# Where the low part of a weight lies in its slot: 2048 instead of 4096 bytes behind the high part, in a float32 attention and feed-forward kernel

## The chip, the cores and the metric

The kernel runs on one core of one Trainium2 chip. The metric is the device time of one execution in microseconds (us); the median of several executions counts, and less is better.

## The reference

`q`, `k`, `v` are float32 of shape (8, 8, 576, 64): batch, heads, sequence, head size. Attention is done in chunks of 64 rows with nothing between chunks. Its result, put together over heads, is the input of a two-layer feed-forward net whose weights are float64.

```python
scores = (1 / sqrt(64)) * q_c @ k_c.T          # per batch, head and chunk: 64 x 64
attn = exp(scores - scores.max(-1)); attn /= attn.sum(-1) + 1e-9
x = (attn @ v_c)  -> (4608, 512)               # tokens x (heads * head size)
h = x @ w_in                                   # w_in (512, 2048)
g = h / (1 + exp(-1.702 * h))
out = (g @ w_out).astype(float32)              # w_out (2048, 512)
```

## The kernel before

**Tiles.** The 4608 tokens are 36 tiles of 128, taken in 9 blocks (`NB`) of 4 tiles (`BT` = 512 tokens). The 2048 inner columns are 16 slices (`NF`) of 128. So the feed-forward net has 144 steps g = (block n, slice j).

**High and low parts.** Every matrix that goes into a feed-forward matmul is split into a high part (the value in the short float form `float32r`) and a low part (what the high part leaves over). A product is then three matmuls: high times low, high times high, low times high. In a step g there are 12 matmuls for `hp` (four chunks `cc` of the 512 input features, three each, lines 606 to 608; the slice of `w_in` is the stationary operand, `x_l` or `x_h` the moving one, 128x512) and 12 for `po` (four token tiles t, three each, lines 641 to 643; `g_l` or `g_h` is stationary, the slice of `w_out` moves, 128x512). For the very first step `h_half` (lines 619 to 621) does the `hp` part in two halves of 256 tokens.

**Which line reads which part.** Line 606 has the high part of `w_in` as stationary operand (moving `x_l`), 607 the same high part (moving `x_h`), 608 the low part (moving `x_h`). Lines 641 and 642 move the high part of `w_out` (stationary `g_l`, `g_h`), 643 moves the low part (stationary `g_h`).

**Weight slots.** There are 16 slots of 8192 bytes per partition, one for each slice j, and they hold the weights for the whole run. The slices j of `w_in` and `w_out` arrive as raw float64 words in the slot (`load`), are turned into float32 in a scratch tile `wtmp` (ScalarE at lines 172 and 176, VectorE at 181, 182 and 188), and then ScalarE writes the high parts into the slot (`part_h`, line 193) and VectorE the low parts (`part_l`, line 196). This is done 16 times, between 28.8 and 119 us of the profile.

**Order.** A planner (`Plan`) sets the order of all instructions from costs, ranks and needs that stand in `plan.add` calls; the order is fixed when the program is built. Within an engine instructions run in that order. The attention of later tiles is slipped in between feed-forward steps. While PE (TensorE's matmuls) runs one matmul, PEld (its weight load) loads the stationary operand of the next.

**After the matmuls.** ScalarE computes g in place in PSUM (line 627) and its high part (628), VectorE the low part (632); at the end of a block the four `po` tiles go to SBUF (lines 650 and 652) and out.

Of the kernel before, what the change touches and what calls it, by code (L numbers as in the profile page):

```python
# [9 lines left out]
F32 = mybir.dt.float32  # L10
F32R = mybir.dt.float32r
# [3 lines left out]
AF = mybir.ActivationFunctionType  # L15
# [83 lines left out]
def tile_chunk_attention_ffn(  # L99
# [9 lines left out]
    nc = tc.nc  # L109
# [4 lines left out]
    P = 128  # L114
    CH = 64
    NP = H // 2
    NCC = DM // P
# [11 lines left out]
    const = ctx.enter_context(tc.tile_pool(name="const", bufs=1))  # L129
# [14 lines left out]

    wt, w_raw, w_tmp = {}, {}, {}

    def slot_user(j):

        return divmod(NF - 1 - j, 2)

    def plan_w(j):
        rank = 0.986 * j - 3.0

        def words():
            word = lambda t, i: w_raw[j].bitcast(t).rearrange("p (n w) -> p n w", w=2)[:, :, i]
            return word(F32, 1), word(I32, 1), word(I32, 0), word(U32, 0)

        def load(part):  # L160
            if part == 0:
                w_raw[j] = const.tile([P, 1024], I64, tag=f"w{j}", name=f"raw_{j}")
                nc.sync.dma_start(  # L163
                    w_raw[j][:, :512].rearrange("p (cc f) -> p cc f", cc=NCC),
                    w_in[:, j * P : (j + 1) * P].rearrange("(cc p) f -> p cc f", p=P),
                )
            else:
                nc.sync.dma_start(w_raw[j][:, 512:], w_out[j * P : (j + 1) * P, :])  # L168

        def scale():  # L170
            hf, hi, li, lu = words()
            nc.scalar.activation(hf, hf, AF.Copy, scale=2.0**-112)  # L172

        def low():
            hf, hi, li, lu = words()
            nc.scalar.activation(li, lu, AF.Copy, scale=2.0**-29)

        def high():
            hf, hi, li, lu = words()
            w_tmp[j] = tmp = more.tile([P, 1024], I32, tag="wtmp", name=f"wtmp_{j}")  # L180
            nc.vector.tensor_scalar(tmp, hi, 3, None, op0=ALU.logical_shift_left)
            nc.vector.scalar_tensor_tensor(
                tmp, hi, -(2**31), tmp, op0=ALU.bitwise_and, op1=ALU.bitwise_or
            )

        def join():
            hf, hi, li, lu = words()
            nc.vector.tensor_tensor(w_tmp[j], w_tmp[j], li, op=ALU.add)
            w_raw.pop(j)

        def part_h():
            wt[j] = const.tile([P, 2, 1024], F32R, tag=f"w{j}", name=f"w_{j}")
            nc.scalar.activation(wt[j][:, 0, :], w_tmp[j].bitcast(F32), AF.Copy)

        def part_l():
            nc.vector.tensor_tensor(  # L196
                wt[j][:, 1, :],
                w_tmp.pop(j).bitcast(F32),
                wt[j][:, 0, :].bitcast(F32),
                op=ALU.subtract,  # L200
            )

        u, kind = slot_user(j)
        need = [f"{('s', 'xp')[kind]}_{u}"] if u < TB else []
        e = lambda n: f"{n}_{j}"
        plan.add(DMA, 1.6, rank - 5.5, lambda: load(0), need=need, make=e("rawi"), take=[f"w{j}"])
        plan.add(DMA, 1.6, rank - 5.5, lambda: load(1), need=[e("rawi")], make=e("raw"))
        plan.add(ACT, 1.1, rank, scale, need=[e("raw")], make=e("wsc"))
        plan.add(ACT, 1.1, rank, low, need=[e("wsc")], make=e("wlow"))
        plan.add(DVE, 1.95, rank, high, need=[e("wsc")], make=e("whigh"), take=["tmp"])  # L210
        plan.add(DVE, 1.25, rank, join, need=[e("whigh"), e("wlow")], make=e("wj"))
        plan.add(ACT, 1.05, rank - 3.5, part_h, need=[e("wj")], make=e("wh"))
        plan.add(DVE, 1.25, rank - 2, part_l, need=[e("wh")], make=e("w"), give=["tmp"])


# [372 lines left out]
    def plan_ffn(g):  # L588
        n, j = divmod(g, NF)
# [8 lines left out]
        def h_pe(half):  # L598
            if half == 0:
                h_t[g] = ps_h.tile([P, BT], F32, tag="hp", name=f"hp_{g}")  # L600
            hp = h_t[g]
            w = wt[j][:, :, :512].rearrange("p w (cc f) -> p w cc f", cc=NCC)
            for cc in range(2 * half, 2 * half + 2):
                wh, wl = w[:, 0, cc, :], w[:, 1, cc, :]
                xh, xl = x_h[n][:, cc, :], x_l[n][:, cc, :]
                nc.tensor.matmul(hp, wh, xl, start=cc == 0, stop=False)  # L606
                nc.tensor.matmul(hp, wh, xh, start=False, stop=False)  # L607
                nc.tensor.matmul(hp, wl, xh, start=False, stop=cc == NCC - 1)  # L608

        def h_half(half):  # L610
            if half == 0:
                h_t[g] = ps_h.tile([P, BT], F32, tag="hp", name=f"hp_{g}")
            c = slice(half * BT // 2, (half + 1) * BT // 2)
            hp = h_t[g][:, c]
            w = wt[j][:, :, :512].rearrange("p w (cc f) -> p w cc f", cc=NCC)
            for cc in range(NCC):
                wh, wl = w[:, 0, cc, :], w[:, 1, cc, :]
                xh, xl = x_h[n][:, cc, c], x_l[n][:, cc, c]
                nc.tensor.matmul(hp, wh, xl, start=cc == 0, stop=False)
                nc.tensor.matmul(hp, wh, xh, start=False, stop=False)  # L620
                nc.tensor.matmul(hp, wl, xh, start=False, stop=cc == NCC - 1)
# [11 lines left out]

        def o_pe(t):
            gh, gl = g_t[g]
            w = wt[j][:, :, 512:]
            if j == 0:
                po_t[(n, t)] = ps_o.tile([P, DM], F32, tag=f"po{t}", name=f"po_{n}_{t}")
            po = po_t[(n, t)]
            c = slice(t * P, t * P + P)  # L640
            nc.tensor.matmul(po, gl[:, c], w[:, 0, :], start=j == 0, stop=False)  # L641
            nc.tensor.matmul(po, gh[:, c], w[:, 0, :], start=False, stop=False)  # L642
            nc.tensor.matmul(po, gh[:, c], w[:, 1, :], start=False, stop=j == NF - 1)  # L643
# [19 lines left out]
        if g == 0:  # L663
            plan.add(
                PE, 1.37, g - 0.2, lambda: h_half(0), need=[need[0], "xl_0", "xl_1"], make=ev("h0"), take=["hp"]
            )
            plan.add(PE, 1.37, g - 0.2, lambda: h_half(1), need=[ev("h0"), "xl_2", "xl_3"], make=ev("h"))
        else:
            plan.add(PE, 1.37, g - 0.2, lambda: h_pe(0), need=need, make=ev("h0"), take=["hp"])
            plan.add(PE, 1.37, g - 0.2, lambda: h_pe(1), need=[ev("h0")], make=ev("h"), give=last)  # L670
        plan.add(ACT, 1.18, g - 5, g_hi, need=[ev("h")], make=ev("gh"), take=["g"], table="gelu")
        plan.add(DVE, 0.69, g - 5, g_lo, need=[ev("gh")], make=ev("gl"), give=["hp"])
        for t in range(TB):
            po = [f"po{t}"] if j == 0 else []
            plan.add(
                PE, 0.69, g + 2.5, lambda t=t: o_pe(t), need=[ev("gl"), f"w_{j}"]
                + ([f"o_{g - 1}_{t}"] if j else [])
                + ([f"o_{g}_{i}" for i in range(t)] if t == TB - 1 else []),
                make=f"o_{g}_{t}", take=po, give=["g"] if t == TB - 1 else [],
            )  # L680
            if j == NF - 1:
                eng = ACT if t % 2 == 0 else DVE
                tag = ob_tag(t)
                plan.add(
                    eng, 0.6, g - 1, lambda t=t: o_out(t), need=[f"o_{g}_{t}"],
                    make=f"ob_{n}_{t}", take=[tag], give=[f"po{t}"],
                )
                plan.add(
                    DMA, 0.8, g - 20, lambda t=t: o_store(t), need=[f"ob_{n}_{t}"],
                    make=f"st_{n}_{t}", give=[tag],  # L690
                )
# [52 lines left out]
```

## Time and profile before

| | |
|---|---|
| time, median of 3 runs | 889.74 us (889.12 to 889.91) |
| the profiled execution's own time | 889.83 us |
| its span | 888.1 us, 14202 instructions |
| PE busy | 870.6 us (98%), 5882 matmuls |
| VectorE (DVE) busy | 389.8 us (44%) |
| ScalarE (ACT) busy | 317.6 us (36%) |
| GpSimd (POOL) busy | 32.4 us (4%) |
| granted TensorE clock | 0.992 over the span |

A row of the groups reads: line, engine, operation, what it writes <- what it reads, shapes, count | busy us, mean ns of one | idle time of the engine before it and what ended it. A row of the timeline reads: start us, length us, engine, line, operation. The length of a matmul runs from its start to a modelled end, and matmuls overlap: the distance from one start to the next is the pace of the engine.

### The profile page before, as it was taken

How to read it: one execution, taken by the hardware profiler on the slowest of the kernel's cores; microseconds unless marked ns; L12 is line 12 of the kernel's file. 1: busy time of each engine (PE TensorE's matmuls, PEld its weight loads, DVE VectorE, ACT ScalarE, POOL GpSimd, SP SyncE). 2: the span in 40 equal slices, each digit the busy share in tenths (PEclk: the TensorE clock that was granted, in tenths of full speed). 3: DMA queues.
4: the chain of work that ended last, by engine and by line, in shares of the span. 5: the costliest groups of instructions: out<-in, count | busy, mean ns of one | idle time of the engine just before them, and what ended most of it. 6: DMA issues, size and time to landing. Idle time of an engine off the chain costs nothing.

```text
span 888.1 us, 14202 instructions
## 1 busy us (share of the span) xinstructions
PE 870.6 (98%) x5882; PEld 705.6 (79%) x5882; DVE 389.8 (44%) x511; ACT 317.6 (36%) x459; POOL 32.4 (4%) x24
## 2 busy tenths in 40 slices
PE   6799999999999999999999999999999999999998
PEld 5587888888888888888888888888888888888886
DVE  5899975277716153433535171617151411111111
ACT  3999653253423223232423241324232322222221
POOL 1000000011000000000000000000000000000000
PEclk9699999999999999999999999999999999999999
DMA  9995244233442313221222031102010110001001
GB/s 238 311 323 169 47 73 98 38 54 67 82 86 54 54 25 76 45 48 25 69 39 49 16 92 25 25 1 71 2 25 1 32 40 1 0 1 48 1 0 48
DMA packets 194592, 55.47 MB, mean 62 GB/s; under 512 B 179680, under 2 KB 187872, under 8 KB 194528
## 3 DMA queue, kind: packets, MB, share of 16 engines
q1 hardware_dynamic: 194528, 54.57, 26.3%
q8 instruction: 46, 0.75, 0.4%
q14 instruction: 18, 0.15, 0.1%
HBM read 45.09 MB, written 9.44 MB: 61 GB/s over the span
## 4 chain that ended last, share of the span: by engine, by line
PE 94%; SPq 2%; DMA 2%; ACT 1%; issue 0%; DVE 0%; ACTq 0%
PE po L641 16%; PE po L642 15%; PE po L643 15%; PE hp L608 15%; PE hp L607 15%; PE hp L606 15%; PE s L443 2%; PE x L503 2%; SPq L231 1%; DMA raw<-in_moe_w_in_dram 1%; DMA rows<-in_k_dram 1%; ACT raw L172 0%; PE qkTp L410 0%; SPq L168 0%; SPq L163 0%
## 5 line engine op out<-in xcount | busy, mean ns | idle before, releaser
L632 DVE TENSOR_TENSOR g_l<-hp,g_h 128x512 fp32r<-128x512 f32 x144 | 99.3, 690 | 413.3 <-ACT g_h L628 412.7
L641 PE MATMUL po<-w,g_l 128*128 128x512 f32 x576 | 232.1, 403 | 0.1
L628 ACT ACTIVATE g_h<-hp 128x512 fp32r<-128x512 f32 x144 | 86.3, 599 | 404.3 <-PE po L643 403.6
L642 PE MATMUL po<-w,g_h 128*128 128x512 f32 x576 | 227.7, 395 | 0.0
L643 PE MATMUL po<-w,g_h 128*128 128x512 f32 x576 | 227.7, 395 | 0.0
L608 PE MATMUL hp<-x_h,w 128*128 128x512 f32 x572 | 225.2, 394 | 0.0
L607 PE MATMUL hp<-x_h,w 128*128 128x512 f32 x572 | 223.9, 391 | 0.0
L606 PE MATMUL hp<-x_l,w 128*128 128x512 f32 x572 | 223.9, 391 | 0.0
L643 PEld LDWEIGHTS po<-w,g_h 128*128 128x128 f32 x576 | 108.6, 189 | 26.3
L641 PEld LDWEIGHTS po<-w,g_l 128*128 128x128 f32 x576 | 108.2, 188 | 25.4 <-DVE g_l L632 0.9
L606 PEld LDWEIGHTS hp<-x_l,w 128*128 128x128 f32 x572 | 107.8, 189 | 25.0
L642 PEld LDWEIGHTS po<-w,g_h 128*128 128x128 f32 x576 | 109.0, 189 | 23.5
L607 PEld LDWEIGHTS hp<-x_h,w 128*128 128x128 f32 x572 | 107.4, 188 | 25.1
L608 PEld LDWEIGHTS hp<-x_h,w 128*128 128x128 f32 x572 | 107.3, 188 | 23.6 <-DVE w L196 0.2
L627 ACT ACTIVATE hp<-hp 128x512 f32<-128x512 f32 x144 | 84.3, 585 | 72.6 <-PE hp L608 67.6
L490 DVE STREAM_TRANSPOSE eT<-e 32x512 f32<-32x512 f32 x112 | 78.7, 702 | 21.0 <-PE x L503 17.2
L470 POOL TENSOR_TENSOR e<-e,r 128x1024 f32<-128x1024 f32 x14 | 26.7, 1906 | 611.4 <-DVE r L466 325.5
L425 DVE STREAM_TRANSPOSE qkT<-raw 128x1024 f32<-128x1024 f32 x28 | 34.7, 1241 | 13.8 <-PE s L443 11.3
L515 ACT ACTIVATE x_h<-x 128x512 fp32r<-128x512 f32 x32 | 17.5, 595 | 33.2 <-PE x L503 33.1
L459 ACT ACT_TABLE_LOAD x16 | 20.5, 1283 | 19.0 <-DVE e L456 18.3
L463 DVE TENSOR_REDUCE z<-e 128x16 f32<-128x1024 f32 x16 | 19.5, 1218 | 9.5 <-ACT e L459 8.8
L443 PEld LDWEIGHTS s<-qkT 64*64 64x64 f32 x1024 | 18.2, 135 | 5.8 <-issue 5.8
(64 smaller groups left out, 412.2 us busy)
## 6 DMA issues: line engine op xcount, KB each, us to landing
out_dram<-ob SPq DMA_DIRECT2D x36, 256.0 KB, 2.1
raw<-in_moe_w_in_dram SPq DMA_DIRECT2D x16, 512.0 KB, 7.3
raw<-in_moe_w_out_dram SPq DMA_DIRECT2D x16, 512.0 KB, 8.0
v<-in_v_dram SPq DMA_DIRECT2D x28, 256.0 KB, 3.3
raw<-in_q_dram SPq DMA_DIRECT2D x144, 32.0 KB, 2.1
raw<-in_k_dram SPq DMA_DIRECT2D x144, 32.0 KB, 2.1
raw<-in_q_dram SPq DMA_DIRECT2D x48, 24.0 KB, 1.9
raw<-in_k_dram SPq DMA_DIRECT2D x48, 24.0 KB, 1.9
```

Source lines behind the costliest of these rows:

```text
L425: nc.vector.transpose(st["tr"][:, i].rearrange("p n (t j) -> p (n t) j", j=32), st["raw"][:, i].rearrange("p n t j -> p (n t) j"),)
L443: nc.tensor.matmul(o, tr[r, 0, n, cols], tr[r, 1, n, cols], start=True, stop=True)
L490: nc.vector.transpose(st["et"][po : po + 32, :, 32 * a : 32 * a + 32], st["e"][pi : pi + 32, :, 32 * b : 32 * b + 32],)
L606: nc.tensor.matmul(hp, wh, xl, start=cc == 0, stop=False)
L607: nc.tensor.matmul(hp, wh, xh, start=False, stop=False)
L608: nc.tensor.matmul(hp, wl, xh, start=False, stop=cc == NCC - 1)
L627: nc.scalar.activation(h_t[g], h_t[g], AF.Gelu_apprx_sigmoid)
L628: nc.scalar.activation(gh, h_t[g], AF.Copy)
L632: nc.vector.tensor_tensor(gl, h_t.pop(g), gh.bitcast(F32), op=ALU.subtract)
L641: nc.tensor.matmul(po, gl[:, c], w[:, 0, :], start=j == 0, stop=False)
L642: nc.tensor.matmul(po, gh[:, c], w[:, 0, :], start=False, stop=False)
L643: nc.tensor.matmul(po, gh[:, c], w[:, 1, :], start=False, stop=j == NF - 1)
```

## The change

A slot held, in this order, the high part of the `w_in` slice, the high part of the `w_out` slice, the low part of the `w_in` slice, the low part of the `w_out` slice, 2048 bytes each. Now it holds high `w_in`, low `w_in`, high `w_out`, low `w_out`. So the low part of `w_in` moves from byte 4096 to 2048 of the slot, the high part of `w_out` from 2048 to 4096; the other two stay.

```diff
         def part_h():
-            wt[j] = const.tile([P, 2, 1024], F32R, tag=f"w{j}", name=f"w_{j}")
-            nc.scalar.activation(wt[j][:, 0, :], w_tmp[j].bitcast(F32), AF.Copy)
+            wt[j] = const.tile([P, 2, 2, 512], F32R, tag=f"w{j}", name=f"w_{j}")
+            nc.scalar.activation(wt[j][:, :, 0], w_tmp[j].bitcast(F32).rearrange("p (m n) -> p m n", m=2), AF.Copy)
 
         def part_l():
             nc.vector.tensor_tensor(
-                wt[j][:, 1, :],
-                w_tmp.pop(j).bitcast(F32),
-                wt[j][:, 0, :].bitcast(F32),
+                wt[j][:, :, 1],
+                w_tmp.pop(j).bitcast(F32).rearrange("p (m n) -> p m n", m=2),
+                wt[j][:, :, 0].bitcast(F32),
                 op=ALU.subtract,
             )
...
         def h_pe(half):          # and the same edit in h_half
-            w = wt[j][:, :, :512].rearrange("p w (cc f) -> p w cc f", cc=NCC)
+            w = wt[j][:, 0].rearrange("p w (cc f) -> p w cc f", cc=NCC)
...
         def o_pe(t):
-            w = wt[j][:, :, 512:]
+            w = wt[j][:, 1]
```

In the built program every engine has the same instructions in the same order with the same waits, and all tiles start at the same addresses as before. What differs: the 16 instructions of `part_h` and the 16 of `part_l` write (and `part_l` reads) two pieces of 512 elements, 4096 bytes apart, where they wrote 1024 in one run; and 1732 matmuls have another operand address: 1152 (lines 641 and 642) of the moving operand, 580 (lines 608 and 621) of the stationary one. A blank line in the new file moves its later lines by one.

More of the change, by code (lines that the diff above doesn't have):

```diff
@@ L614, in h_half @@
             hp = h_t[g][:, c]
-            w = wt[j][:, :, :512].rearrange("p w (cc f) -> p w cc f", cc=NCC)
+            w = wt[j][:, 0].rearrange("p w (cc f) -> p w cc f", cc=NCC)
             for cc in range(NCC):
```

## The prediction

> **What bounds the kernel now.** I read the page first, for the span and the chain that ended last, and its groups.
>
> ```profile
> span 888.1 us, 14202 instructions
> ...
> PE 94%; SPq 2%; DMA 2%; ACT 1%; issue 0%; DVE 0%; ACTq 0%
> ...
> L632 DVE TENSOR_TENSOR g_l<-hp,g_h 128x512 fp32r<-128x512 f32 x144 | 99.3, 690 | 413.3 <-ACT g_h L628 412.7
> L641 PE MATMUL po<-w,g_l 128*128 128x512 f32 x576 | 232.1, 403 | 0.1
> L628 ACT ACTIVATE g_h<-hp 128x512 fp32r<-128x512 f32 x144 | 86.3, 599 | 404.3 <-PE po L643 403.6
> L642 PE MATMUL po<-w,g_h 128*128 128x512 f32 x576 | 227.7, 395 | 0.0
> L643 PE MATMUL po<-w,g_h 128*128 128x512 f32 x576 | 227.7, 395 | 0.0
> L608 PE MATMUL hp<-x_h,w 128*128 128x512 f32 x572 | 225.2, 394 | 0.0
> L607 PE MATMUL hp<-x_h,w 128*128 128x512 f32 x572 | 223.9, 391 | 0.0
> L606 PE MATMUL hp<-x_l,w 128*128 128x512 f32 x572 | 223.9, 391 | 0.0
> ```
>
> PE carries 94% of the chain, and its six feed-forward lines have no idle time ahead of them (the last column is 0.0 or 0.1 us over hundreds of matmuls). Next came the windows, to see whether that holds in the stretch where weights are still being prepared.
>
> ```profile
> 60.00:80.00 20.00, 20.00 (x92) 16.41 (x91) 18.88 (x23) 18.84 (x22) 0.00 (x0) 1.00 0.88 269
> 80.00:100.00 20.00, 19.69 (x207) 15.48 (x205) 18.36 (x21) 15.44 (x20) 0.00 (x0) 1.00 0.21 37
> ...
> 700.00:800.00 100.00, 100.00 (x491) 81.19 (x490) 19.70 (x30) 23.86 (x41) 0.00 (x0) 1.00 0.04 13
> ```
>
> The columns after the length are the busy time of PE, PEld, DVE, ACT and POOL, then the clock. PE is busy for all of 60 to 80 us and for 19.69 of the next 20, while DVE and ACT are nearly full (18.88 and 18.84 of 20): preparing the weights is hidden, but with little to spare. Late in the run (700 to 800) DVE and ACT are a fifth busy and PE sets the pace alone. The waits of the weight load from 36 us to the end show how little the other engines hold it up (the three rows with another engine in them):
>
> ```profile
> PEld po L641 <- DVE g_l L632: 0.9, 2, 0.6
> PEld qkTp L410 <- ACT eT L481: 0.7, 1, 0.7
> ...
> PEld hp L608 <- DVE w L196: 0.2, 1, 0.2
> ```
>
> That is 1.8 us in all, four waits. So the time is the pace of the matmuls, and the question is whether an operand's address has a say in it. For this the timeline of PE near the end, where one step g follows the other without attention between:
>
> ```profile
> 863.33 0.39 PE L606 MATMUL hp<-x_l,w 128*128 128x512 f32 x1
> 863.55 0.39 PE L607 MATMUL hp<-x_h,w 128*128 128x512 f32 x1
> 863.78 0.39 PE L608 MATMUL hp<-x_h,w 128*128 128x512 f32 x1
> 864.01 0.39 PE L606 MATMUL hp<-x_l,w 128*128 128x512 f32 x1
> 864.24 0.39 PE L607 MATMUL hp<-x_h,w 128*128 128x512 f32 x1
> 864.46 0.40 PE L608 MATMUL hp<-x_h,w 128*128 128x512 f32 x1
> 864.69 0.40 PE L641 MATMUL po<-w,g_l 128*128 128x512 f32 x1
> ...
> 870.25 0.40 PE L641 MATMUL po<-w,g_l 128*128 128x512 f32 x1
> ```
>
> One step of 24 matmuls takes 870.25 - 864.69 = 5.56 us, 231.7 ns each. The `hp` lines run at (864.46 - 863.33)/5 = 226 ns from start to start. The `po` lines run slower; the last stretch of the run, with `po` matmuls alone, shows how:
>
> ```profile
> 875.81 0.40 PE L641 MATMUL po<-w,g_l 128*128 128x512 f32 x1
> 876.05 0.40 PE L642 MATMUL po<-w,g_h 128*128 128x512 f32 x1
> ...
> 877.44 0.40 PE L642 MATMUL po<-w,g_h 128*128 128x512 f32 x1
> 877.68 0.40 PE L643 MATMUL po<-w,g_h 128*128 128x512 f32 x1
> ...
> 879.07 0.40 PE L643 MATMUL po<-w,g_h 128*128 128x512 f32 x1
> 879.31 0.40 PE L641 MATMUL po<-w,g_l 128*128 128x512 f32 x1
> ...
> 880.69 0.40 PE L641 MATMUL po<-w,g_l 128*128 128x512 f32 x1
> 880.93 0.40 PE L642 MATMUL po<-w,g_h 128*128 128x512 f32 x1
> ```
>
> From 875.81 to 880.69 stand 21 steps in 4.88 us: 232.4 ns each, 6.4 more than the `hp` pace. Each pair above is a long one of 0.24 us (0.23 in the unquoted rows between). A long one comes every seventh matmul (1.63, 1.63 and 1.62 us apart), and it falls on line 641, then 642, then 643, then 641 again. So whatever lengthens `po` matmuls goes by a rhythm of its own; it does not stick to the line, though line 643 reads its moving weights 4096 bytes further on in the slot than 641 and 642, and 642's stationary operand lies in another tile than 641's.
>
> **The change part by part.** The order, the waits and the counts stay, so there are two things to price.
>
> First, the 1732 matmuls with another operand address. For the 1152 of lines 641 and 642, the moving weights go from byte 2048 of the slot to 4096. The nearest comparison in this trace is line 642 against line 643: the same stationary `g_h`, the same output, moving weights from byte 2048 against byte 6144. Their means are 395 and 395 ns over 576 each. The rounding leaves half a nanosecond either way: 1152 x 0.5 ns = 0.6 us, gain or loss. For the 580 of lines 608 and 621, the stationary low part goes from byte 4096 to 2048. The nearest comparison is line 607 against 608: the same moving `x_h`, stationary weights from byte 0 against byte 4096: 391 and 394 ns. If the 3 ns were the address, a place nearer to the high part might win or lose up to as much: 580 x 3 ns = 1.7 us either way. The timeline speaks against it: the 608 at 863.78, which another `hp` matmul follows, is 0.39 us long like its neighbours, and the 0.40 us stand at 864.46, where a `po` matmul follows. I take 0 for both, since in the rows nearest to the change an offset of 4096 bytes in the same slot shows nothing.
>
> The Trainium skill has a rule here: SBUF — State Buffer, section "Who interferes with whom", gives PE two independent read ports (moving operand, weight load) and says that PE never waits on anyone; TensorE: Matmul & The Clock Gate, section "Back-to-back issue gap", gives N/2.4 + 2.5 ns from start to start, about 216 ns for 512 columns. By these pages no address could matter and the rivals A and B below would have no chance. The trace does not quite agree with them: 226 and 232.4 ns are 10 and 16 ns above that figure with PE never idle, so something does hold the stream up, and the rivals keep a chance.
>
> Second, the 16 instructions of `part_h` (ACT) and the 16 of `part_l` (DVE) handle two pieces of 512 where they had one run of 1024. The rows for what they cost now, and for a tile written in pieces:
>
> ```profile
> L518 DVE TENSOR_TENSOR x_l<-x,x_h 128x512 fp32r<-128x512 f32 x32 | 20.6, 684 | 2.9 <-ACT x_h L515 2.8
> ...
> L196 DVE TENSOR_TENSOR w<-wtmp,w 128x1024 fp32r<-128x1024 f32 x16 | 19.4, 1215 | 0.4 <-ACT w L193 0.4
> ...
> L515 ACT ACTIVATE x_h<-x 128x512 fp32r<-128x512 f32 x32 | 17.5, 595 | 33.2 <-PE x L503 33.1
> ...
> L193 ACT ACTIVATE w<-wtmp 128x1024 fp32r<-128x1024 f32 x16 | 16.8, 1057 | 0.7 <-DVE wtmp L188 0.7
> ```
>
> Line 518 writes `x_l` in four pieces of 128 with a stride, line 632 writes `g_l` in one run of 512: 684 against 690 ns. On ACT line 515 against line 628: 595 against 599 ns. Pieces cost nothing there, so I take 0 (at best 16 x 6 ns = 0.1 us less). The upper end: if each piece cost as much as an instruction of its own, DVE would pay 2 x 690 - 1215 = 165 ns, 2.6 us in 16, and ACT 2 x 599 - 1057 = 141 ns, 2.3 us in 16. What hides them is PE's own work; only the four waits above (1.8 us) could grow, and from DVE and ACT nearly full at 60 to 80 us I let at most DVE's whole 2.6 us come through.
>
> The sum: 889.83 us (the profiled execution's own time, its span of 888.1 and 1.7 around it) + 0 + 0. This execution lies 0.09 above the median of the runs, 889.74, so I forecast 889.7 us. With the bounds of the matmuls (0.6 and 1.7 us, either way) the likeliest case runs from 887.4 to 892.0, but both ends at once need every bound at its worst; I count within 0.2% (888.0 to 891.5) as this case. About 0.2% is also what a measurement of this kernel can tell from no change, as the three runs already lie 0.8 us apart.
>
> **The rivals.**
>
> A, faster: the `po` matmuls lose their rhythm. They run 6.4 ns above the `hp` pace, and 1152 of the 1728 get another moving address. If these fell to 226 ns, 1152 x 6.4 ns = 7.4 us would go: 882.3 us. For it: the two kinds differ in nothing but operands and addresses, with PE never idle. Against it: the long matmul wanders over all three lines, so the slot offset is not what makes it. Chance 0.09.
>
> B, slower: the reverse, on the `hp` side. While PE streams `x_h`, PEld reads the low part from its new place at byte 2048; if this meets the stream as badly as the weight loads of `po` do, the 572 steps of line 608 go from 226 to 232.4 ns: 572 x 6.4 = 3.7 us, 893.4 us, and up to 1716 x 6.4 = 11 us (900.7) if the rhythm spreads over all of `hp`. It decides from 3 ns on each matmul of line 608 (1.7 us). For it: byte 2048 of a slot has never been a stationary address. Against it: the rows from 863.33 on are chunks 2 and 3, whose stationary operands start at bytes 1024 and 1536 (high) and 5120 and 5632 (low) of the slot, and they run alike. Chance 0.07.
>
> C, slower: two pieces are dear on DVE, which is 94% busy from 60 to 80 us, and `w` or `g_l` comes late to PE: up to 2.6 us, 892.3 us. Against it: lines 518 and 632. Chance 0.04.
>
> **How the numbers follow.** The forecast has what is left, 0.80, and lies within 0.2%; A is the chance of faster, 0.09; B and C that of slower, 0.11. For the range I take 888.0 to 892.0 us: nearly all of the forecast's case and the lower part of C; A and B, 0.16, stay outside.
>
> **What would show it.** Right: lines 606 to 608 and 641 to 643 (one number higher in the new file) with the same means within 1 ns, a step of 5.56 us near the end, the long `po` matmul still every seventh, `part_l` and `part_h` at 1215 and 1057 ns. A would show `po` means nearer 391 and a step near 5.51 us; B the line of the low `w_in` part well over 394 ns; C `part_l` near 1380 ns and new waits of PEld for `w` or `g_l` before 119 us. The forecast is wrong if the step near the end leaves 5.55 to 5.57 us, since 144 steps make 1.4 us of each hundredth.

## The result, and the profile after

| | before | after |
|---|---|---|
| median of 12 runs each | 889.93 us | 889.94 us |
| span of the profiled execution | 888.1 us | 888.2 us |

The ratio is 1.0002, with a 95% interval of 0.9993 to 1.0011: no difference that these runs can tell. The groups of the changed kernel (its lines are one number higher: 607 to 609 for `hp`, 642 to 644 for `po`, 194 for `part_h`, 197 for `part_l`):

```profile
L642 PE MATMUL po<-w,g_l 128*128 128x512 f32 x576 | 232.1, 403 | 0.1
L643 PE MATMUL po<-w,g_h 128*128 128x512 f32 x576 | 227.7, 395 | 0.0
L644 PE MATMUL po<-w,g_h 128*128 128x512 f32 x576 | 227.7, 395 | 0.0
L609 PE MATMUL hp<-x_h,w 128*128 128x512 f32 x572 | 225.3, 394 | 0.0
L607 PE MATMUL hp<-x_l,w 128*128 128x512 f32 x572 | 223.9, 392 | 0.0
L608 PE MATMUL hp<-x_h,w 128*128 128x512 f32 x572 | 223.9, 391 | 0.0
...
L197 DVE TENSOR_TENSOR w<-wtmp,w 128x1024 fp32r<-128x1024 f32 x16 | 19.3, 1214 | 0.5 <-ACT w L194 0.5
...
L194 ACT ACTIVATE w<-wtmp 128x1024 fp32r<-128x1024 f32 x16 | 16.8, 1059 | 0.7 <-DVE wtmp L189 0.7
```

All eight means are within 2 ns of before. The timeline of PE near the end shows the step and the rhythm:

```profile
864.82 0.40 PE L642 MATMUL po<-w,g_l 128*128 128x512 f32 x1
...
870.38 0.40 PE L642 MATMUL po<-w,g_l 128*128 128x512 f32 x1
...
875.94 0.40 PE L642 MATMUL po<-w,g_l 128*128 128x512 f32 x1
876.18 0.40 PE L643 MATMUL po<-w,g_h 128*128 128x512 f32 x1
...
877.56 0.40 PE L643 MATMUL po<-w,g_h 128*128 128x512 f32 x1
877.80 0.40 PE L644 MATMUL po<-w,g_h 128*128 128x512 f32 x1
```

A step takes 870.38 - 864.82 = 5.56 us as before, and the long `po` matmul (0.24 us) still comes every seventh, first on the line of the high part with `g_l`, then on the next. The waits of PEld from 36 us on with another engine in them:

```profile
PEld po L642 <- DVE g_l L633: 0.9, 2, 0.6
PEld qkTp L411 <- ACT eT L482: 0.7, 1, 0.7
PEld hp L609 <- DVE w L197: 0.4, 1, 0.4
PEld s L444 <- DVE wtmp L189: 0.4, 1, 0.4
```

The wait for a low part of `w` went from 0.2 to 0.4 us, and one wait of the attention (`s`, 0.4 us) now has DVE's name. The other two stayed, and in all it is 2.4 us where it was 1.8.

### The profile page after: what moved, and what is told of

The parts are those of the page before. It is cut to its first block, busy times and chain, and to the rows that moved or that the text cites. A ratio compares the mean times of both kernels' runs of the same rounds, so it can differ in the third digit from the quotient of the medians.

```text
span 888.2 us, 14202 instructions
## 1 busy us (share of the span) xinstructions
PE 870.5 (98%) x5882; PEld 705.5 (79%) x5882; DVE 389.7 (44%) x511; ACT 317.5 (36%) x459; POOL 32.3 (4%) x24
## 4 chain that ended last, share of the span: by engine, by line
PE 94%; SPq 2%; DMA 2%; ACT 1%; issue 0%; DVE 0%; ACTq 0%
PE po L642 16%; PE po L643 15%; PE po L644 15%; PE hp L609 15%; PE hp L608 15%; PE hp L607 15%; PE s L444 2%; PE x L504 2%; SPq L232 1%; DMA raw<-in_moe_w_in_dram 1%; DMA rows<-in_k_dram 1%; ACT raw L173 0%; PE qkTp L411 0%; SPq L169 0%; SPq L164 0%
## 5 line engine op out<-in xcount | busy, mean ns | idle before, releaser
L460 ACT ACT_TABLE_LOAD x16 | 20.5, 1283 | 19.1 <-DVE e L457 18.3
```

## The experiments

The first question was whether the prediction's reason holds: that the pace of the matmuls is blind to where their operands lie. Each kernel ran beside the kernel before, whose median was 889.6 to 889.7 us in these groups of runs; ratios are against it. The padding tiles are never read; they move what is allocated after them.

**The g tiles moved by 128 bytes.** In the built program the weight slots and `x_h`, `x_l` start 128 bytes past a multiple of 512, `g_h` and `g_l` at a multiple of 512.

```diff
         def g_hi():
+            if g == 0:
+                two.tile([P, 16], F32, tag="pad", name="pad")   # 2 buffers x 64 bytes
             gh = two.tile([P, BT], F32R, tag="gh", name=f"g_h_{g}")
```

> The kernel before, with the g_h and g_l tiles 128 bytes further on (their start is now 128 bytes past a multiple of 512, as that of the weight slots and of x is; it was a multiple of 512). Theory (the pace of the matmuls is blind to operand addresses): no change, 889.9 us, po lines at 395 and 403 ns, a long one every seventh. Rival (the rhythm of the po matmuls comes from the distance of the two operands within 512 bytes): the po matmuls fall from 232.4 to 226 ns from start to start, 1728 x 6.4 ns = 11 us less, 879 us.

Measured: 875.01 us, ratio 0.9838 (0.9821 to 0.9854). The theory fell. The timeline of PE and four of the groups:

```profile
850.33 0.39 PE L643 MATMUL po<-w,g_l 128*128 128x512 f32 x1
850.56 0.39 PE L644 MATMUL po<-w,g_h 128*128 128x512 f32 x1
850.78 0.39 PE L645 MATMUL po<-w,g_h 128*128 128x512 f32 x1
...
855.77 0.39 PE L643 MATMUL po<-w,g_l 128*128 128x512 f32 x1
```
```profile
L643 PE MATMUL po<-w,g_l 128*128 128x512 f32 x576 | 227.7, 395 | 0.0
...
L606 PE MATMUL hp<-x_l,w 128*128 128x512 f32 x572 | 223.4, 391 | 0.0
L608 PE MATMUL hp<-x_h,w 128*128 128x512 f32 x572 | 222.8, 389 | 0.1
L607 PE MATMUL hp<-x_h,w 128*128 128x512 f32 x572 | 222.7, 389 | 0.0
```

The rhythm is gone: every matmul, `po` or `hp`, follows the last after 0.22 to 0.23 us, and a step takes 855.77 - 850.33 = 5.44 us, 226.7 ns for each of 24. It gained 14.7 us where the rival gave 11, since the `hp` matmuls that follow `po` had been held up too: lines 607 and 608 fell from 391 and 394 ns to 389, and the step near the end is 0.12 us shorter, of which the 12 `po` matmuls at 6.4 ns make 0.08. So the place of an operand does count, but not by 2048 bytes.

**The x tiles moved by 128 bytes.**

```diff
+            if n == 0:
+                two.tile([P, 16], F32, tag="pad", name="pad")
             x_h[n] = two.tile([P, NCC, BT], F32R, tag="xh", name=f"x_h_{n}")
             x_l[n] = two.tile([P, NCC, BT], F32R, tag="xl", name=f"x_l_{n}")
+            if n == 0:
+                two.tile([P, 48], F32, tag="pad2", name="pad2")
```

> The kernel before, with the x_h and x_l tiles 128 bytes further on and the g tiles 512 bytes further on, so that for the hp matmuls the moving operand is 128 bytes off the stationary one modulo 512, as it is for the po matmuls, and for po nothing changes modulo 512. Theory (blind to addresses): no change, 889.9 us, hp lines at 391, 391 and 394 ns. Rival (distance within 512 bytes): hp goes to the pace of po, 1716 x 6.4 ns = 11 us more, 901 us.

Measured: 887.79 us, ratio 0.9978 (0.9969 to 0.9987). Neither came: it is 1.9 us faster. Its groups (610 to 612 are `hp`, 645 to 647 `po`), and rows from the last stretch, with `po` alone:

```profile
L645 PE MATMUL po<-w,g_l 128*128 128x512 f32 x576 | 230.8, 401 | 0.1
L647 PE MATMUL po<-w,g_h 128*128 128x512 f32 x576 | 227.1, 394 | 0.0
L646 PE MATMUL po<-w,g_h 128*128 128x512 f32 x576 | 225.5, 391 | 0.0
L611 PE MATMUL hp<-x_h,w 128*128 128x512 f32 x572 | 224.8, 393 | 0.0
L610 PE MATMUL hp<-x_l,w 128*128 128x512 f32 x572 | 224.4, 392 | 0.0
L612 PE MATMUL hp<-x_h,w 128*128 128x512 f32 x572 | 224.0, 392 | 0.5 <-DVE w L196 0.5
```
```profile
875.82 0.40 PE L647 MATMUL po<-w,g_h 128*128 128x512 f32 x1
876.06 0.39 PE L645 MATMUL po<-w,g_l 128*128 128x512 f32 x1
876.29 0.40 PE L646 MATMUL po<-w,g_h 128*128 128x512 f32 x1
...
881.42 0.40 PE L647 MATMUL po<-w,g_h 128*128 128x512 f32 x1
```

Lines 610 and 611 got longer (391 to 392 and 393) as the rival says, but line 612 got shorter (394 to 392), and so did `po` (line 646: 395 to 391), though its own operands kept their distance modulo 512. Beside the stream without a rhythm (391, 389 and 389 ns with `g` moved) `hp` is held up here, by 1 to 4 ns; it was held up behind `po` in the kernel before as well. In the last stretch a long `po` matmul comes every second time, not every seventh, and 24 matmuls take 881.42 - 875.82 = 5.60 us, 233.3 ns each where it was 232.4. So the price of a distance is not a constant per matmul: it depends on what ran before, or on more of the addresses than their distance modulo 512. Which of the two is open.

**The preparation of the weights made dearer.** The changed kernel, with each `part_h` and `part_l` in two instructions:

```diff
-            nc.scalar.activation(wt[j][:, :, 0], w_tmp[j]....rearrange("p (m n) -> p m n", m=2), AF.Copy)
+            for m in range(2):
+                nc.scalar.activation(wt[j][:, m, 0], w_tmp[j].bitcast(F32)[:, 512 * m : 512 * m + 512], AF.Copy)
...
+            for m in range(2):      # the same for the subtraction of part_l
```

> The changed kernel with part_h and part_l each issued as two instructions of 512 elements, one for each matrix: the price that the prediction put at the upper end of two pieces. Theory (the weights' preparation is hidden behind the matmuls): DVE +16 x 165 ns = 2.6 us busy, ACT +16 x 141 ns = 2.3 us, the time within 0.5 us of 889.9. Rival (DVE and ACT are the bound at 60 to 80 us): up to 2.6 us more, 892.5 us, with new waits of PEld for w or g_l before 119 us.

Measured: 889.81 us, ratio 1.0002 (0.9993 to 1.0011). Its groups and its longest wait of PEld for a feed-forward operand:

```profile
L200 DVE TENSOR_TENSOR w<-wtmp,w 128x512 fp32r<-128x512 f32 x32 | 20.4, 681 | 0.0
...
L195 ACT ACTIVATE w<-wtmp 128x512 fp32r<-128x512 f32 x32 | 18.3, 628 | 0.7 <-DVE wtmp L189 0.7
```
```profile
PEld po L642 <- DVE g_l L633: 1.2, 2, 0.8
```

DVE is busy 1.1 us longer than in the changed kernel (20.4 against 19.3) and ACT 1.5 us (18.3 against 16.8), less than the bounds of 2.6 and 2.3, since instructions in a row overlap a little (32 x 681 ns are 21.8 us, in 20.4 us of busy time). The wait for `g_l` grew from 0.9 to 1.2 us, and the time stayed. So the preparation has room beside the matmuls for this much; C's whole price of 2.6 us was not put on it.

**The low part behind the high part in every 512 bytes.**

```diff
-            wt[j] = const.tile([P, 2, 2, 512], F32R, tag=f"w{j}", name=f"w_{j}")
+            wt[j] = const.tile([P, 8, 2, 128], F32R, tag=f"w{j}", name=f"w_{j}")
...
-            w = wt[j][:, 1]
+            w = wt[j][:, 4:].rearrange("p m w f -> p w m f")
```

> The change taken further: the low part lies right behind the high part for each 512 bytes (128 columns) instead of each 2048. Stationary low parts start 512 bytes behind the high ones; the moving slice of w_out is read in four pieces of 512 bytes, 1024 apart. Theory (blind to addresses and to pieces of 512 bytes): no change, 889.9 us, and part_h and part_l at 1057 and 1215 ns though they write eight pieces. Rival (a jump in the moving operand's addresses costs the stream): each of three jumps at least 1 cycle, 0.4 ns, in 1728 matmuls: 2.2 us or more, 892 us or more.

Measured: 889.78 us, ratio 1.0001 (0.9991 to 1.0010); `part_l` 1214 ns and `part_h` 1057 ns, the matmul means as before to the nanosecond. Moves by a multiple of 512 bytes, and a moving operand in four pieces, cost nothing here.

The second question: which distance counts, and between which places? (A distance modulo 256 or 512 is what is left of it after taking off multiples of that number.)

**All operands at a multiple of 512 bytes.**

```diff
     make_identity(nc, ident)
+    const.tile([P, 96], F32, tag="pad0", name="pad0")       # and the pad of 128 bytes ahead of g_h
```

> The kernel before with 384 bytes of padding ahead of the weight slots and 128 ahead of the g tiles: weight slots, x and g all start at a multiple of 512 bytes. Theory (what counts is how far the two operands of a matmul and its neighbours are apart modulo 512): 875 us, 227 ns from start to start everywhere, as with g alone moved by 128. Rival (the absolute start counts, 128 past a multiple of 512 being a good one and 0 a bad one): all 3444 matmuls run in the rhythm, 232.4 ns: about 900 us.

Measured: 873.54 us, ratio 0.9818 (0.9804 to 0.9833). The rhythm is gone here too, so the absolute start does not make it. This is the fastest version of all, 16.2 us under the kernel before. Its median is 1.5 us under the run with g alone moved. The first `hp` and the last `po` matmul, here and then there:

```profile
31.30 0.58 PE L620 MATMUL hp<-x_l,w 128*128 128x256 f32 x1
...
868.37 0.39 PE L646 MATMUL po<-w,g_h 128*128 128x512 f32 x1
```
```profile
32.07 0.58 PE L619 MATMUL hp<-x_l,w 128*128 128x256 f32 x1
...
869.14 0.39 PE L645 MATMUL po<-w,g_h 128*128 128x512 f32 x1
```

From the one to the other it is 837.07 us in both, so the pace of the matmuls is the same. The 0.8 us between these two executions (874.25 and 875.01 us) lie ahead of the feed-forward net; why, and what makes the rest of the 1.5 us, the runs do not show.

**The g tiles moved by 64 bytes** (`two.tile([P, 8], ...)` as the pad).

> The kernel before with the g tiles 64 bytes further on: 64 bytes past a multiple of 512, weight slots and x stay 128 past. Theory (any distance that is not a multiple of 512 brings the rhythm): 887 to 892 us. Rival (only distances of 128 bytes and more count, or it goes by the size of the distance): 875 to 882 us.

Measured: 879.68 us, ratio 0.9886 (0.9871 to 0.9900): between the two. Its `po` groups:

```profile
L643 PE MATMUL po<-w,g_l 128*128 128x512 f32 x576 | 229.5, 398 | 0.0
L644 PE MATMUL po<-w,g_h 128*128 128x512 f32 x576 | 226.9, 394 | 0.0
L645 PE MATMUL po<-w,g_h 128*128 128x512 f32 x576 | 224.4, 390 | 0.0
```

At a distance of 64 bytes the hold-up is smaller than at 128 and sticks to the line: 398, 394 and 390 ns, where the distance of 128 bytes had 403, 395 and 395, and no distance (g moved by 128) has 395, 389 and 390.

**The g tiles moved by 256 bytes** (pad `[P, 32]`): the moving weights now start 128 bytes short of `g`, not 128 past.

> The kernel before with the g tiles 256 bytes further on: the moving slice of w_out now starts 128 bytes short of the stationary g modulo 512, where it started 128 past it. Theory (any distance that is not a multiple of 512 brings the rhythm): 887 to 892 us. Rival (only a moving operand ahead of the stationary one is held up): 875 us.

Measured: 889.71 us, ratio 1.0000 (0.9990 to 1.0009), with the means of before (403, 395, 395). 128 short is as bad as 128 past: either the sign does not count, or the distance counts modulo 256.

**The g tiles moved by 384 bytes** (pad `[P, 48]`): 256 bytes apart tells those two apart.

> The kernel before with the g tiles 384 bytes further on: the moving slice of w_out and the stationary g are 256 bytes apart modulo 512 (0 modulo 256). 128 past and 128 short gave the same time, 889.7 us. Theory (the distance counts modulo 256): 875 us, no rhythm. Rival (modulo 512, and 128 past and 128 short are alike because only the size of the distance counts): 889 us or more, as 256 is then the largest distance there is.

Measured: 874.84 us, ratio 0.9834 (0.9819 to 0.9848). So the distance counts modulo 256: 256 bytes apart is as good as 0, and 128 short as bad as 128 past.

**The changed kernel with the g tiles moved by 128 bytes.**

> The changed kernel with the g tiles 128 bytes further on: the change on the base where the rhythm is gone. Theory (multiples of 512 bytes do not count, with the rhythm or without it): 875.0 us, the same as the kernel before with g moved by 128, within 0.1%. Rival (the slot order has a small effect that the rhythm covered): a difference of 1 us or more.

Measured: 874.95 us, ratio 0.9834 (0.9820 to 0.9849), against 875.01 us for the slot order of before with the same pad. Slot order makes no difference without the rhythm either.

**The edit's own operand, moved by an odd multiple of 128.** On the base with g moved by 128 bytes the low part of `w_in` goes 128 bytes off in 14 slots; the lists give the places in floats, by turns because a slot of 8320 bytes shifts the next one by 128.

```diff
+    def at(j):                       # high parts, low part of w_in, low part of w_out
+        if j in (6, 7): return 0, 1024, 1536
+        if odd[j]: return 544, 0, 1568
+        return 0, 1568, 1024
...
-                wh, wl = w[:, 0, cc, :], w[:, 1, cc, :]
+                wh, wl = wth[:, cc, :], wtl[:, cc, :]      # from at(j)
```

> On the base without the rhythm (the kernel before with the g tiles 128 bytes further on, 875.0 us): in 14 of the 16 slots the low part of w_in alone is moved to a place 128 bytes off modulo 256 (slots of 8320 bytes, the other three parts stay at their residue; part_l is issued as two instructions), so 508 matmuls of the line that reads the low part of w_in as stationary operand are changed, nearly the same ones as in the change under study, but by an odd multiple of 128 in place of 2048. Theory (the distance counts modulo 256): slower, 508 x 6 ns = 3 us, 878 us, between 876.5 and 880. Rival (only the alignment of g counts, whatever it is by): 875.0 us.

Measured: 879.67 us, ratio 0.9889 (0.9873 to 0.9906), 4.7 us above the base, whose interval (0.9821 to 0.9854) ends below it. The timeline of PE (621 to 623 are `hp`, 623 the low part; 661 is `po`), then the first `hp` and the last `po` matmul:

```profile
845.45 0.39 PE L621 MATMUL hp<-x_l,w 128*128 128x512 f32 x1
845.68 0.40 PE L622 MATMUL hp<-x_h,w 128*128 128x512 f32 x1
845.91 0.40 PE L623 MATMUL hp<-x_h,w 128*128 128x512 f32 x1
...
846.60 0.40 PE L623 MATMUL hp<-x_h,w 128*128 128x512 f32 x1
846.84 0.39 PE L661 MATMUL po<-w,g_l 128*128 128x512 f32 x1
```
```profile
29.95 0.58 PE L636 MATMUL hp<-x_l,w 128*128 128x256 f32 x1
...
873.32 0.39 PE L663 MATMUL po<-w,g_h 128*128 128x512 f32 x1
```

The six `hp` matmuls take 846.84 - 845.45 = 1.39 us, 231.7 ns each, against 226.7 on the base, and it is lines 622 and 623 that grew (0.40 us long): the matmul under which the displaced weights are loaded and the one that uses them. From the first `hp` matmul to the last `po` it takes 873.32 - 29.95 = 843.37 us, 6.3 us more than the 837.07 of the base. The 14 slots in 9 blocks are 126 steps with 12 `hp` matmuls each, so that is 4.2 ns for each of these, over the whole run. Of the 6.3 us 2.1 come back, as the first `hp` matmul starts at 29.95 us in place of 32.07; why it does these runs do not show. So the operands that the edit moves by 2048 bytes do cost time once they are moved by 128.

**The low part right behind the high part in every 4 bytes**, on the same base: the limit of this kind of layout.

```diff
-            wt[j] = const.tile([P, 2, 2, 512], F32R, tag=f"w{j}", name=f"w_{j}")
+            wt[j] = const.tile([P, 2, 512, 2], F32R, tag=f"w{j}", name=f"w_{j}")
...
-            w = wt[j][:, 1]
+            w = wt[j][:, 1].rearrange("p f w -> p w f")
```

> The changed kernel on the base without the rhythm (875.0 us), with the low part right behind the high part for each element: every second float of a slot is a high part, stationary and moving weights are read with a step of 8 bytes, part_h and part_l write with that step. Theory (pace goes by the start modulo 256 alone, and a start 4 bytes off hardly counts): within 2 us of 875. Rival (the density of the reads counts: the 32 cycles that a matmul takes beyond its 512 columns are for reading the stationary 512 bytes, and spread over 1024 bytes these are 64): 1716 x 13.3 ns = 23 us more for hp, and for po half of its reads spread too: 898 us or more.

Measured: 1273.26 us, ratio 1.4313 (1.4291 to 1.4334). The theory fell. The rival's number (898 us or more) held, but its mechanism did not:

```profile
L646 PE MATMUL po<-w,g_h 128*128 128x512 f32 x576 | 366.5, 636 | 0.0
L645 PE MATMUL po<-w,g_h 128*128 128x512 f32 x576 | 363.7, 631 | 0.0
L644 PE MATMUL po<-w,g_l 128*128 128x512 f32 x576 | 361.0, 627 | 0.0
L607 PE MATMUL hp<-x_l,w 128*128 128x512 f32 x572 | 231.4, 405 | 0.0
L608 PE MATMUL hp<-x_h,w 128*128 128x512 f32 x572 | 225.4, 394 | 0.0
L609 PE MATMUL hp<-x_h,w 128*128 128x512 f32 x572 | 224.9, 393 | 0.0
```

A moving operand read with a step of 8 bytes makes a `po` matmul about 240 ns longer (627 to 636 against 389 to 395 on the base), which is more than its whole pace of 227. In the last stretch, with `po` alone, 29 of them take from 1253.44 to 1266.59 us, 453 ns each from start to start: half speed. The stationary operand with the same step, which the rival had for the cause, costs `hp` 4 to 14 ns only, the most on line 607, which also follows the slow `po` matmuls.

## Why the prediction was right

**The bound.** PE set the time, as read from the chain and the windows; the run with the dearer preparation shows that DVE and ACT have room for 1.1 and 1.5 us more of this work, though they look full at 60 to 80 us.

**The 1732 matmuls, taken at 0.** Right in size: `hp` 392, 391 and 394 ns, `po` 403, 395 and 395. The comparison that carried it (line 642 against 643, 607 against 608: 4096 bytes apart in one slot, no difference) was a fair one, but the sentence drawn from it was too wide. What these runs support is: whether matmuls are held up depends on the distance of their operands modulo 256 bytes, and 2048 and 4096 are multiples of 256. The prediction had a row for 4096 bytes only and took 2048 to be like it; that this was safe, it could not know, and here it had some luck. The half nanosecond and the 3 ns that were kept as bounds were both nothing; the 3 ns of line 608 belonged to the rhythm, as they went with it (389 ns).

**"A rhythm of its own."** This step failed. The rhythm of the `po` matmuls does not stick to a line, as the prediction said, but it is made by an address: 128 bytes between the weight slots and the `g` tiles. It goes when these are 0 or 256 bytes apart (875.0 and 874.8 us) and stays at 128 past and 128 short. The prediction also read both paces, 226 and 232.4 ns, as held up. The runs bear out only the second: 226.7 ns is the pace of the stream where the rhythm is gone. This failed step did not enter the forecast, since the edit does not touch the 128 bytes.

**Rival A** had the right suspicion, since `po` and `hp` differed in an address and not in their kind, and `po` can be brought to 226.7 ns. But the edit moves that address by 2048 bytes, a multiple of 256. **Rival B** had a real mechanism as well: displaced low parts do hold up `hp`, by 6.3 us from the first matmul to the last where it gave 3.7, on two lines of three and not on one; but only for a distance that is no multiple of 256. **Rival C** was wrong by the rows it was held against, as `part_l` stayed at 1214 ns, and the run with two instructions bears that out.

The Trainium skill, SBUF — State Buffer, section "Who interferes with whom", has PE never wait on anyone and its two read ports independent. Here a matmul's pace goes from 226.7 to 232.4 ns by the place of what the two read, with next to no wait for another engine (1.8 us in the kernel before); the measurement decides. The runs do not show how the two reads meet, only that they do.

## What to carry to other kernels

Before pricing a move of data, ask by how many bytes it moves modulo a small power of two: here back-to-back float32r matmuls were held up where the stationary and the moving operands started at different remainders modulo 256 bytes, and the kernels with all of them at one remainder were the fastest (873.5 to 875.0 us). A few small tiles in the same pool (`m`, `z` and `r`, 64 bytes each, in two buffers) had put `g` 128 bytes off and cost 14.7 us; a pad of 128 bytes gives them back, and it is the uneven spacing of like matmuls in the timeline that shows it. Evidence that an offset does nothing holds for that offset and its multiples, not for offsets.

## What the runs showed of the hardware that was not expected

- The distance of the stationary and the moving operands modulo 256 bytes decides whether a stream of matmuls is held up: 226.7 ns at 0 (5.44 us for 24); at 128 bytes 232.4 ns for `po` alone, with a long one every seventh; at 64 bytes a smaller hold-up that stays on the same lines (879.7 us against 875.0 and 889.7).
- How much a distance of 128 bytes costs is not fixed: with both `hp` and `po` at 128 the kernel was 1.9 us faster than with `po` alone there (887.8 us), and the long `po` matmul came every second time. That is open.
- A moving float32r operand with a step of 8 bytes runs at half speed (453 ns from start to start against 226.7), a stationary one loses 4 to 14 ns.
